# A 64-byte touch of batch 1's rows ahead of their load, in a transformer block on one core

## The chip, the core and the metric

The kernel runs on one core of a Trainium2 chip. The time is device microseconds of one execution. Each execution comes with a state, "fast" or "slow"; a lone execution on one core is "unknown". A profile is one further execution, taken by the hardware profiler; its span is about 2 us shorter than the device time. The sessions ran on different chips (the record names 12, 5, 10 and 0), so traces of different sessions can also differ by the chip.

## The reference, cut to what matters

```python
B, N, D = 2, 256, 1152                      # x: bf16[2, 256, 1152], c: bf16[2, 1152]
mod = (silu(c) @ w_mod).reshape(B, 6, 1, D) # shift_a, scale_a, gate_a, shift_m, scale_m, gate_m
h = layernorm(x) * (1 + scale_a) + shift_a
# q, k, v = h @ wqkv; attention with 2 heads; x = x + gate_a * (a @ wo)
# x + gate_m * (gelu(h2 @ w_fc1) @ w_fc2), h2 the second layernorm, modulated
```

Only the first line of the block matters here: x and c must arrive, x is normalised, transposed and scaled, and then the K projection can begin.

## The kernel before

x is held as four tiles of 128 partitions. Partition p of a batch holds rows 2p and 2p+1, so tiles 0 and 1 are the first and second row of each pair of batch 0, tiles 2 and 3 those of batch 1. A row is 2304 B, a pair 4608 B of contiguous memory.

```python
x_v = x.rearrange("b (p l) d -> p b l d", l=TPB)      # TPB = 2 rows to a partition
...
nc.scalar.dma_start(c_sb[:], c_v)                     # ACT's queue
for t in (0, 1, 3, 2):                                # SP's queue
    nc.sync.dma_start(x_sb[:, t, :], x_v[:, t // TPB, t % TPB, :])
... # then w_scale_a and w_k in pieces on SP's queue
nc.scalar.add_instruction(mybir.InstLoadActFuncSet(...))   # ACT's table load
warm(2, pwarm)                                        # TensorE matmuls on zeros
nc.tensor.transpose(pc[:], c_sb[:], ...)
nc.scalar.activation(sig[:], pc[:], ACT.Exp, scale=-1.0)   # silu(c), finished on DVE
...
warm(7, pwarm)
act_stats(0)                    # two ACT passes over tile 0: sum and sum of squares
for j in range(NPD): stats_piece(1, j)       # tile 1's statistics on DVE
act_mean_eps(0)
act_root(0)                     # inverse roots of tiles 0 and 1 on ACT: Ln, Ln, Exp
nc.scalar.activation(rstd1[:, 1:2], mv1[:, 1, 1:2], ACT.Ln, bias=eps_t[:], scale=1.0)
root_exp(0, 2)
act_stats(2)                    # two ACT passes over tile 2
for j in range(NPD): stats_piece(3, j)       # tile 3's statistics on DVE
...
norm1(1, 0, CUT); norm1(0, 0, CUT); pt_a = transpose_x([0, 1], BT[0])
act_mean_eps(2); act_root(2); root_exp(2, 3)
...
norm1(2, 0, CUT)
...
transpose_x([0, 1], [2], pt_c, 0)            # "tile 2's transposes" below
```

The kernel's last lines tie the instructions of each engine to the order of the text.

## Time and profile before

| what | before |
|---|---|
| time, median of 3 runs | 243.72 us (243.39 to 243.89) |
| span of the profile | 241.4 us |
| TensorE busy | 236.4 us (98%) |
| tile 2's transposes start | 11.03 us |
| x tiles 0, 1, 3, 2 land, us after their issues | 2.9, 3.2, 4.6, 4.9 |

The prediction shows the lines. Read them thus: the chain of waits says what ended last and what it had waited for, back to the start. It is on TensorE from 11.03 us to 238.3 us, so the time is 11.03 us plus a block on TensorE that this change does not edit. "Landing" is the time from the start of an issue until its semaphore says that all of it has arrived.

### The profile page before, as it was taken

The page shows a single profiled execution, that of the slowest core. Times are in us where ns is not written, and L with a number is a line of the kernel's source. Part 1 is how long each engine was busy: PE and PEld are TensorE (multiplying, and loading weights), DVE is VectorE, ACT ScalarE, POOL GpSimd, SP SyncE. Part 2 cuts the span into 40 slices and gives each one's busy share as a digit, 9 for nine tenths or more (in the row PEclk, how much of TensorE's full clock was granted, in tenths as well). Part 3 has the DMA queues.
Part 4 walks back from the last instruction along what each step waited for, and adds up shares of the span by engine and source line. Part 5 has one row for each costly group of instructions (what it writes and reads, how often), then busy time and mean ns, then how long its engine had stood idle before and what let it go on. Part 6 is the DMA issues. An engine that isn't in the chain of part 4 may idle for free.

```text
span 241.4 us, 3978 instructions
## 1 busy us (share of the span) xinstructions
PE 236.4 (98%) x1688; PEld 145.1 (60%) x1698; DVE 91.4 (38%) x193; ACT 59.9 (25%) x121; POOL 28.3 (12%) x47
## 2 busy tenths in 40 slices
PE   8999999999999999999999999999999999999994
PEld 5775444466667665888844444444665566666574
DVE  4842442319325678930003999950010000000001
ACT  6723322307215032770423333222000000000000
POOL 2300000001300324100000000001121111111111
PEclk9999999999999999999999999999999999999999
DMA  6999999997499993739999999999300000000000
GB/s 196 325 317 311 377 366 391 391 391 244 122 331 394 389 274 76 195 65 378 391 391 391 337 326 270 287 327 270 98 16 16 20 16 16 19 18 20 26 21 16
DMA packets 48781, 53.29 MB, mean 221 GB/s; under 512 B 9587, under 2 KB 36475, under 8 KB 48763
## 3 DMA queue, kind: packets, MB, share of 16 engines
q1 hardware_dynamic: 41312, 50.14, 62.5%
q10 hardware_dynamic: 6939, 1.71, 4.6%
q0 software_dynamic: 512, 1.19, 1.8%
q8 instruction: 13, 0.21, 0.4%
q14 instruction: 5, 0.04, 0.1%
HBM read 50.14 MB, written 1.19 MB: 213 GB/s over the span
## 4 chain that ended last, share of the span: by engine, by line
PE 94%; issue 2%; ACT 2%; POOL 1%; DVE 0%; POOLq 0%; DVEq 0%; ACTq 0%
PE pacc L802 29%; PE pacc L746 29%; PE pacc L693 7%; PE pacc L599 7%; PE pq L521 7%; PE pk L280 5%; PE pk L309 2%; PE pa L640 2%; PE ps_s L556 2%; PE pn L416 2%; ACT sink L206 1%; PE pt L264 1%; PE pm L247 1%; PE pg L498 0%; ACT rstd L335 0%
## 5 line engine op out<-in xcount | busy, mean ns | idle before, releaser
L746 PE MATMUL pacc<-hT,w_f 128*128 128x256 bf16 (+1 forms) x427 | 70.3, 325 | 0.3
L802 PE MATMUL pacc<-w_f,gT 128*128 128x384 bf16 (+2 forms) x468 | 70.5, 314 | 0.0
L802 PEld LDWEIGHTS <-gT 128*128 128x128 bf16 x468 | 44.4, 98 | 26.3
L746 PEld LDWEIGHTS <-w_f 128*128 128x128 bf16 x432 | 42.2, 98 | 27.6
L808 DVE TENSOR_TENSOR tmp<-pacc,gate 128x384 f32<-128x384 f32 (+2 forms) x13 | 6.8, 526 | 65.6 <-PE pacc L802 57.0
L778 ACT ACTIVATE gT<-pacc 128x512 bf16<-128x512 f32 x24 | 14.3, 597 | 32.7 <-PE pacc L746 32.7
L469 DVE SCALAR_TENSOR_TENSOR part<-w_gate_m,s,part 128x1152 f32<-128x1152 bf16 x16 | 21.4, 1412 | 0.0
L810 POOL TENSOR_TENSOR o_sb<-tmp,x 128x384 bf16<-128x384 f32 (+1 forms) x12 | 11.7, 972 | 53.9 <-DVE tmp L808 53.9
L693 PE MATMUL pacc<-w_o,big 128*128 128x384 bf16 x108 | 17.9, 326 | 0.0
L521 PE MATMUL pq<-hT,w_q 128*128 128x512 bf16 x79 | 17.7, 379 | 0.1
L599 PE MATMUL pacc<-w_v,hT 128*128 128x384 bf16 x108 | 17.7, 326 | 0.0
L599 PEld LDWEIGHTS <-hT 128*128 128x128 bf16 x108 | 10.5, 98 | 7.1 <-issue 0.2
L693 PEld LDWEIGHTS <-big 128*128 128x128 bf16 x108 | 10.4, 98 | 7.2 <-issue 0.4
L521 PEld LDWEIGHTS <-w_q 128*128 128x128 bf16 x81 | 7.8, 98 | 9.4
L280 PE MATMUL pk<-big,w_k 128*128 128x256 bf16 (+1 forms) x70 | 13.1, 324 | 0.1
L699 POOL TENSOR_TENSOR x<-tmp,x_sb 128x384 f32<-128x384 f32 x8 | 7.3, 912 | 27.0 <-DMA w_scale_m<-in_w_mod_dram 15.0
L467 DVE TENSOR_SCALAR part<-w_gate_m,s 128x1152 f32<-128x1152 bf16 x2 | 1.6, 818 | 21.9 <-DMA w_gate_m<-in_w_mod_dram 21.9
L491 POOL DMA_DIRECT2D gates_dram<-nat_v x2 | 1.1, 534 | 67.7 <-DVE nat_v L489 67.7
L280 PEld LDWEIGHTS <-w_k 128*128 128x128 bf16 x72 | 6.7, 97 | 3.7 <-issue 0.3
L767 ACT ACTIVATE gT<-pacc 128x512 bf16<-128x512 f32 x12 | 6.5, 598 | 9.1 <-PE pacc L746 9.1
L173 PE MATMUL pwarm<-zeros 128*128 128x256 f32 x18 | 7.4, 587 | 1.2 <-DVE eps_t L93 1.2
L512 POOL DMA_DIRECT2D gates_dram<-nat x4 | 2.4, 604 | 49.6 <-DVE nat L509 48.5
(102 smaller groups left out, 165.0 us busy)
## 6 DMA issues: line engine op xcount, KB each, us to landing
w_f<-in_w_fc_dram SPq DMA_DIRECT2D x12, 864.0 KB, 14.1
w_f<-in_w_fc_dram SPq DMA_DIRECT2D x3, 1728.0 KB, 7.9
w_f<-in_w_fc_dram SPq DMA_DIRECT2D x2, 2592.0 KB, 17.4
w_gate_a<-in_w_mod_dram SPq DMA_DIRECT2D x3, 864.0 KB, 12.1
w_v<-in_wqkv_dram SPq DMA_DIRECT2D x3, 864.0 KB, 13.8
w_o<-in_wo_dram SPq DMA_DIRECT2D x3, 864.0 KB, 14.0
w_shift_m<-in_w_mod_dram SPq DMA_DIRECT2D x3, 864.0 KB, 8.6
w_scale_m<-in_w_mod_dram SPq DMA_DIRECT2D x3, 864.0 KB, 13.3
```

The costliest lines, as they stand in the source:

```text
L173: nc.tensor.matmul(dst[:, 0:T // 2], zeros32[:, 0:P], zeros32, start=True, stop=True)
L280: nc.tensor.matmul(pk[m][:, c0:c1], w_k[:, k, m * P:(m + 1) * P], hT0[:, k, c0:c1], start=(k == 0 and c0 == 0), stop=(k == KD - 1), skip_g ...
L469: nc.vector.scalar_tensor_tensor(part[:, b, :], wg[:, k, :], s32[:, k, b:b + 1], part[:, b, :], op0=ALU.mult, op1=ALU.add,)
L521: nc.tensor.matmul(pq[m][:], w_q[:, k, m * P:(m + 1) * P], hT[:, k, :], start=(k == 0), stop=(k == KD - 1), skip_group_check=True,)
L599: nc.tensor.matmul(pacc[:], hT[:, k, t * P:(t + 1) * P], w_v[:, k, pnl * PW:(pnl + 1) * PW], start=(k == 0), stop=(k == KD - 1),)
L693: nc.tensor.matmul(pacc[:], aT[:, k, t * P:(t + 1) * P], w_o[:, k, c0:c1], start=(k == 0), stop=(k == KD - 1),)
L699: (nc.gpsimd if pool_add else nc.vector).tensor_tensor(x1[:, t, c0:c1], tmp[:], x_sb[:, t, c0:c1], op=ALU.add)
L746: nc.tensor.matmul(dst, w_f1[m // KD][:, k, ml * P:(ml + 1) * P], hT[:, k, c0:c1], start=start, stop=(k == KD - 1), **kw,)
L778: nc.scalar.activation(gT[:, m, :], pacc[:], ACT.Gelu_apprx_tanh)
L802: nc.tensor.matmul(pacc[:], gT[:, kk, t * P:(t + 1) * P], w_f2[j][:, r, c0 - n * PW:c0 - n * PW + cw], start=(kk == 0), stop=(kk == KF - 1),)
L808: nc.vector.tensor_tensor(tmp[:], pacc[:], gate_m[:, b, c0:c0 + cw], op=ALU.mult)
L810: (nc.vector if last else nc.gpsimd).tensor_tensor(o_sb[:], tmp[:], x1[:, t, c0:c0 + cw], op=ALU.add)
```

## The change

The intent is that a tiny read of each row pair of batch 1, in good time, makes the full read of those rows (tile 3, then tile 2) quicker.

```diff
     nc.scalar.dma_start(c_sb[:], c_v)
+    touch_x = act.tile([P, 32], BF16, name="touch_x")
+    nc.scalar.dma_start(touch_x[:], x_v[:, 1, 0, 0:32])
     for t in (0, 1, 3, 2):
```

Nothing reads `touch_x`.

## The prediction

> **What bounds the kernel now.** I read the page first, then the chain of waits in order of time, then the timeline of the first 12 us, then DMA traffic in short windows. The page says who is busy:
>
> ```profile
> span 241.4 us, 3978 instructions
> PE 236.4 (98%) x1688; PEld 145.1 (60%) x1698; DVE 91.4 (38%) x193; ACT 59.9 (25%) x121; POOL 28.3 (12%) x47
> PE 94%; issue 2%; ACT 2%; POOL 1%; DVE 0%; POOLq 0%; DVEq 0%; ACTq 0%
> ```
>
> The third line is the chain that ended last: 94% of the span is TensorE. The chain in order of time shows where the change can act:
>
> ```profile
> 6.51 0.29 ACT rstd L335
> ...
> 7.23 1.25 ACT sink L206 x2
> ...
> 10.56 0.42 DVE xn L233
> 10.98 0.05 issue
> 11.03 0.29 PE pt L264 x2
> 11.32 0.44 PE pk L280 x4
> ```
>
> The columns are start, length, what. From 11.03 us, where TensorE transposes the last tile of x, to 238.3 us the chain stays on TensorE, with some nine gaps of 0.05 us. The change touches only the prologue before 11.03 us. A microsecond lost or won at 11.03 is a microsecond at the end; nothing later can multiply it, and only about half a microsecond of gaps could hide it. So the stake is the few tenths by which that start moves.
>
> How x reaches the engines, from the timeline:
>
> ```profile
> 0.73 0.62 ACTq L84 DMA_DIRECT2D c_sb<-in_c_dram  x1
> 0.73 1.81 SPq L86 DMA_DIRECT2D x_sb<-in_x_dram  x4
> 1.39 1.28 ACT L153 ACT_TABLE_LOAD   x1 [1.39 <-PEq L841]
> 3.41 0.19 ACT L178 ACTIVATE sig<-pc 128x18 f32<-128x18 bf16 x1 [0.74 <-PE pc L176]
> 3.63 1.25 ACT L206 ACTIVATE sink<-x_sb 128x1152 f32<-128x1152 bf16 x1
> 4.38 1.48 DVE L193 BATCH_NORM_STATS2 stats<-x_sb 128x6 f32<-128x384 bf16 x3
> 6.22 1.48 DVE L193 BATCH_NORM_STATS2 stats<-x_sb 128x6 f32<-128x384 bf16 x3
> 7.13 1.24 ACT L206 ACTIVATE sink<-x_sb 128x1152 f32<-128x1152 bf16 x1
> ```
>
> The four x tiles are issued in the order 0, 1, 3, 2 about 0.45 us apart, and the tile view gives landings 2.9, 3.2, 4.6 and 4.9 us after issue: about 3.6, 4.4, 6.2 and 7.0 us. Their first readers start at 3.63 (ACT, tile 0), 4.38 (DVE, tile 1), 6.22 (DVE, tile 3) and 7.13 (ACT, tile 2). The landings thus sit within about 0.1 us of the readers, but no wait on x is listed: at each of the four points the reading engine had also just ended its previous work. Both conditions bind together.
>
> **What the Trainium skill says.** Four places bear on it.
> - "DMA: Bandwidth & Descriptors", section "Issuing engines are not separate DMA queues": loads from ACT and SP run on the same 16 engines and interleave. The trace agrees: c's 27 packets on queue q10 (18 rows and, I take it, 9 completion writes) lie among the first x packets on q1. So the touch is no free side channel.
> - The same page, "Queues, rings and completion order": an engine goes round-robin between the rows that have work, packet by packet. No run so far shows the order. By it the touch's 8 packets on each engine cut in among the packets of x tiles 0 and 1 though SP issued those first.
> - The same page, "Latency and other measured facts": HBM access 0.2 us on average, 2 us at high load, and about 0.8 us as the least round trip of a DMA. Here c's issue starts at 0.73 and its packets appear from about 1.6 us: 0.9 us, which fits. No page that I found says that a first read of an HBM row makes later reads of it faster.
> - "ScalarE: Activation LUTs", "What ACT_TABLE_LOAD costs": about 1283 ns for the load. The trace has 1.28 us. It stands right behind the DMA issue on ACT, so the new issue pushes it.
>
> **The change part by part.** It removes nothing. It adds one DMA issue on ACT, 128 reads of 64 B, 8 on each engine, a 64 B tile per partition that nobody reads, and perhaps a faster first read of batch 1's rows. A row pair is 2 x 2304 B = 4608 B, and tile 3 is the first tile to read them, tile 2 the second; likewise tile 0 and tile 1 for batch 0.
>
> *ACT issue.* c's issue took 0.62 us; an x issue of 128 rows on SP took 0.38 to 0.43. Take 0.45 to 0.65. The table load then runs from about 1.9 or 2.0 to 3.2 or 3.3 us. The next ACT instruction started at 3.41 after 0.74 us of idle time, waiting for PE, so the shift is covered with 0.1 to 0.3 us to spare: cost on the path 0. c is ahead on the same queue, and its packets were read by about 1.8 us, before the touch can start (1.4 issue + 0.9 = 2.3 us).
>
> *DMA work added.* c's packets of 256 B: 18 in the window 1.4 to 1.8 us, at a 3.9% share: 0.039 x 16 x 0.4 us / 18 = 14 ns each. If the touch's cost the same, 8 x 14 = 0.11 us on each engine. If each also carries a first-read penalty, more. That penalty I estimate from x's own packets of 2304 B, share x 16 x window / packets:
>
> ```profile
> q1 hardware_dynamic: 25, 0.06, 60.6%
> q1 hardware_dynamic: 74, 0.16, 103.7%
> q1 hardware_dynamic: 38, 0.07, 86.9%
> ```
>
> These are the windows 1.8 to 2.2 us (start of tile 0), 3.0 to 3.4 (tile 1) and 4.6 to 5.0 (tile 3). They give 155, 90 and 146 ns a packet. Batch 1's first reads do look some 60 ns slower than the second reads of batch 0's rows. That is presumably what the change is after. A touch packet could then take up to 14 + 60 = 74 ns, or 0.6 us an engine if nothing overlaps. Small reads should overlap in part; I choose 0.25 us as the delay that tiles 0 and 1 see, out of 0.1 to 0.6.
>
> *What the delay does.* Tile 1 lands at about 4.4 with its reader at 4.38: no slack. DVE's statistics of tile 1 (1.48 us), the aggregate and the small step at 6.05 feed POOL at 6.25, ACT at 6.51, then ACT's passes over tile 2 and DVE's at 10.56, which is the chain shown. Tile 0's delay is partly covered: ACT ended its second pass at 6.37 and started the next at 6.51, 0.14 us. So 0.25 us on tile 1 is about 0.2 us at 11.03.
>
> *What faster rows give back.* If tiles 3 and 2 (0.59 MB, from about 3.75 to 5.95 us by adding up the windows, 2.2 us) ran at tile 1's 369 GB/s they would need 1.6 us: at most 0.6 us earlier, which pays back the added packets and brings the weights behind them earlier. But on the chain it buys nearly nothing. Tile 3's reader is held by DVE until 6.14, tile 2's by ACT's exponential at 7.02: 0.08 and 0.1 us. An earlier tile 3 by itself shortens nothing on tile 1's path. The weights land at 8.98 (first scale chunk, used 9.04) and 9.6 (first K rows); earlier is of use only if TensorE is ready earlier, and it isn't, because it waits for the normalised tiles.
>
> *Sum.* +0.2 from tile 1, 0 from ACT, -0.05 from tile 3 and tile 2: about +0.15 us. 243.72 + 0.15 = 243.87, which I round to **243.9 us**.
>
> **The rivals.**
> 1. The warming works and pays: tiles 3 and 2 and the weights come 0.4 to 0.6 us earlier. For it: 146 against 90 ns a packet. Against it: at 6.22 and 7.13 the readers are bound by their own engines, and ACT's two passes over tile 2 (2.7 us) stay. If tile 1 is undisturbed it makes 243.4 to 243.7.
> 2. The touch is expensive: 64 B reads of cold rows hold their engines, tiles 0 and 1 land 0.6 us later and tile 2 too, since its slack is only 0.1 us. For it: all loads share the engines and tile 1 has no slack. Against it: c's 256 B packets took 14 ns. It makes 244.3 to 244.5.
> 3. The ACT issue is longer than 0.75 us because both queues generate descriptors at once; then the table load ends after 3.41 and the sigmoid of c slips, with DVE behind it, all on the path. c's 0.62 us against 0.38 on SP speaks for some of it. Each 0.1 us over costs 0.1: 243.9 to 244.2.
> 4. Nothing measurable: the touch overlaps entirely, 243.7.
>
> **Range and chances.** The three runs of before span 0.5 us by themselves. The mechanisms give from -0.3 to +0.8. The range that should hold it 8 times in 10 is 243.3 to 244.5. A change of 2% is 4.9 us, several times anything that the prologue can give: the whole stretch in which x is loaded and normalised is 11 us and the change adds 8 KB to it. So faster 0.01, within 2% 0.98, slower 0.01.
>
> **What would show it.** Right: the table load starts about 0.5 us later and the wait for PE before the sigmoid shrinks to 0.1 to 0.3; tile 1's statistics start 0.1 to 0.4 us after 4.38; the transposes of tile 2 start between 11.0 and 11.4 and the rest is shifted as a block. The warming is real if the packets at the start of tile 3 fall from about 146 to near 90 ns and tiles 3 and 2 take clearly under 4.6 and 4.9 us to land. Wrong: transposes of tile 2 starting before 10.9 us, which would mean that the landings, not the engines, set the readers; or after 11.6; or a difference that arises after 11.03 us, where I see no way for it.

## The result, and the profile after

| | before | after |
|---|---|---|
| median of 6 runs | 243.49 us (243.23 to 243.89) | 243.31 us (243.10 to 244.06) |
| ratio | | 0.9995, 95% interval 0.9978 to 1.0011 |
| span of the profile | 241.4 us | 241.4 us |

A ratio is the mean time of one kernel's fast runs over the mean of the other's of the same rounds, so it is not quite the ratio of the medians. The interval holds both the 0.15 us that I had forecast (1.0006) and a gain of that size. Time alone can say no more; what follows reads the start of the steady work in the traces.

The page of the changed kernel:

```profile
span 241.4 us, 3989 instructions
PE 236.6 (98%) x1698; PEld 144.9 (60%) x1698; DVE 91.5 (38%) x193; ACT 59.9 (25%) x121; POOL 28.3 (12%) x47
PE 94%; issue 2%; ACT 2%; POOL 1%; DVE 0%; POOLq 0%; DVEq 0%; ACTq 0%
```

The instruction counts differ by more than the one issue because some matmul records can be missing from a trace (1688 and 1698 here). Its timeline, in the lines that answer to those of before (the first two numbers are start and length):

```profile
1.38 0.36 ACTq L86 DMA_DIRECT2D touch_x<-in_x_dram  x1
1.78 1.28 ACT L155 ACT_TABLE_LOAD   x1 [1.78 <-issue]
3.41 0.19 ACT L180 ACTIVATE sig<-pc 128x18 f32<-128x18 bf16 x1 [0.35 <-PE pc L178]
4.42 1.48 DVE L195 BATCH_NORM_STATS2 stats<-x_sb 128x6 f32<-128x384 bf16 x3
6.10 1.47 DVE L195 BATCH_NORM_STATS2 stats<-x_sb 128x6 f32<-128x384 bf16 x3
7.18 1.24 ACT L208 ACTIVATE sink<-x_sb 128x1152 f32<-128x1152 bf16 x1
```

ACT's table load moved from 1.39 to 1.78 us; the sigmoid stayed at 3.41, and ACT's wait before it shrank from 0.74 to 0.35 us. Tile 1's statistics start 0.04 us later, tile 3's 0.12 us earlier, tile 2's 0.05 us later. In this trace tiles 3 and 2 landed 4.1 and 4.4 us after issue, each 0.5 us sooner than in the trace of before. The chain did not use it:

```profile
7.27 1.25 ACT sink L208 x2
...
10.60 0.42 DVE xn L235
11.03 0.05 issue
11.07 0.28 PE pt L266 x2
11.36 0.44 PE pk L282 x4
```

Tile 2's transposes start at 11.07 us against 11.03. ACT could begin tile 2 only when its own roots of tiles 0 and 1 were done. TensorE's first transposes, of tiles 1 and 0, came 0.13 us earlier (8.48 against 8.61 us); TensorE then sat idle for 0.30 us before tile 2's transposes, which ate that gain.

Where the touch's packets went is seen in the DMA traffic of 3.4 to 3.8 and 3.8 to 4.2 us (queue q10, which is ACT's; packets, MB, share of 16 engines' time):

```profile
q10 hardware_dynamic: 59, 0.00, 10.0%
q10 hardware_dynamic: 85, 0.00, 14.3%
```

These are all 144 packets that q10 gained: 128 reads of 64 B and 16 packets of 4 B, presumably completion writes (the packed trace lists the sizes). They took 0.143 x 16 x 0.4 us / 85 = 10.8 ns each, 0.1 us an engine in all. And they were served at 3.4 to 4.2 us. By 3.8 us q1 had moved 277 packets, and two tiles of x have 288 if each has 144 like the touch. So the touch ran at the end of tile 1 and the start of tile 3, which is the order of the issues (1.17 us tile 1, 1.38 touch, 1.62 tile 3), and at most some tenths of a microsecond ahead of the load that it should help.

### The profile page after: what moved, and what is told of

Its sections match the earlier page's. It is cut to its first block, busy times and chain, and to the rows that moved or that the text cites. A ratio compares the mean times of both kernels' runs of the same rounds, so it can differ in the third digit from the quotient of the medians.

```text
span 241.4 us, 3989 instructions
## 1 busy us (share of the span) xinstructions
PE 236.6 (98%) x1698; PEld 144.9 (60%) x1698; DVE 91.5 (38%) x193; ACT 59.9 (25%) x121; POOL 28.3 (12%) x47
## 4 chain that ended last, share of the span: by engine, by line
PE 94%; issue 2%; ACT 2%; POOL 1%; DVE 0%; POOLq 0%; DVEq 0%; ACTq 0%
PE pacc L748 29%; PE pacc L804 29%; PE pacc L695 7%; PE pacc L601 7%; PE pq L523 7%; PE pk L282 5%; PE pk L311 2%; PE pa L642 2%; PE ps_s L558 2%; PE pn L418 2%; ACT sink L208 1%; PE pt L266 1%; PE pm L249 1%; PE pg L500 0%; ACT rstd L337 0%
## 5 line engine op out<-in xcount | busy, mean ns | idle before, releaser
L748 PE MATMUL pacc<-hT,w_f 128*128 128x256 bf16 (+1 forms) x432 | 70.5, 326 | 0.0
L804 PE MATMUL pacc<-w_f,gT 128*128 128x384 bf16 (+2 forms) x468 | 70.5, 314 | 0.0
```

Of the source, the lines that this page charges most:

```text
L748: nc.tensor.matmul(dst, w_f1[m // KD][:, k, ml * P:(ml + 1) * P], hT[:, k, c0:c1], start=start, stop=(k == KD - 1), **kw,)
L804: nc.tensor.matmul(pacc[:], gT[:, kk, t * P:(t + 1) * P], w_f2[j][:, r, c0 - n * PW:c0 - n * PW + cw], start=(kk == 0), stop=(kk == KF - 1),)
```

## The experiments

The packets in 4.6 to 5.0 us, which the prediction took for the start of tile 3, gave the same picture. It shows the line of before (146 ns a packet); after has 108.9% x 6.4 us / 80 = 87 ns:

```profile
q1 hardware_dynamic: 80, 0.16, 108.9%
```

Two explanations stood against each other. **Warming**: the touch makes tiles 3 and 2 land 0.5 us sooner, and the order on ACT hides it. **Scatter**: landings differ by that much from run to run anyway. All fourteen traces with their prologues, so that they can be compared at once (landings in us after issue; the rest from the span's start):

| kernel | tile 3 lands | tile 2 lands | ACT starts tile 2 | tile 2's transposes | span |
|---|---|---|---|---|---|
| before | 4.6 | 4.9 | 7.13 | 11.03 | 241.4 |
| before_again | 4.3 | 4.8 | 7.17 | 11.06 | 241.7 |
| pool_only (no touch) | 4.3 | 4.8 | 6.97 | 11.08 | 241.4 |
| quiet (no touch at the start) | 4.1 | 5.0 | 7.10 | 11.01 | 241.8 |
| after | 4.1 | 4.4 | 7.18 | 11.07 | 241.4 |
| after_again | 4.4 | 5.6 | 7.74 | 11.66 | 242.0 |
| after_3 | 4.1 | 4.7 | 7.34 | 11.23 | 241.6 |
| pool_touch | 4.5 | 4.8 | 7.01 | 10.92 | 241.2 |
| touch_b0 | 3.9 | 5.0 | 7.19 | 11.09 | 241.4 |
| touch16 | 4.4 | 4.7 | 7.19 | 11.09 | 241.4 |
| touch3 | 4.7 | 5.1 | 7.67 | 11.57 | 242.3 |
| touch_first | 3.9 | 4.4 | 7.75 | 11.65 | 242.0 |
| touch_first2 | 3.9 | 4.5 | 7.76 | 11.96 | 242.3 |
| touch_first_b0 | 4.5 | 5.1 | 7.89 | 11.79 | 242.1 |

Span less the start of tile 2's transposes is 230.3 to 230.8 us in every row, while the start itself moves from 10.92 to 11.96: the start of the steady work sets the end to within half a microsecond, whatever the kernel. That half has causes of its own. In before_again, with 230.6, the chain does not lead back to x at all but to a piece of the weights behind it:

```profile
8.09 7.39 DMA w_scale_a<-in_w_mod_dram
15.52 0.60 PE pm L247 x18
```

In before these matmuls had started at 15.27 us.

### Both kernels again, unchanged

> The kernel before, unchanged, for the scatter of the landings. Warming theory (T1: the touch makes batch 1's rows faster to read): x tiles 3 and 2 land again 4.6 and 4.9 us after issue, within 0.15, and the packets in 4.6 to 5.0 us take 130 to 150 ns. Chance theory (T0: the 0.5 us between the two traces is scatter from run to run): one of the landings differs by 0.3 us or more from those. Transposes of tile 2 start at 11.03 within 0.1.

> The changed kernel, unchanged. T1: tiles 3 and 2 land 4.1 and 4.4 us after issue, within 0.15. T0: anything between 4.0 and 4.9. Transposes of tile 2 at 11.07 within 0.1 under both.

The repeat of before took 243.45 us, that of the changed kernel 243.77, and before on the same chip 243.98 (single runs, state unknown). In the repeat of the changed kernel tile 2 landed after 5.6 us, 1.2 us later than in its first trace, and this time it is on the chain:

```profile
2.11 5.61 DMA x_sb<-in_x_dram
7.72 0.02 issue
7.74 1.36 ACT sink L208 x2
...
11.66 0.29 PE pt L266 x2
```

The chain now leads back to the load of tile 2 itself (issued at 2.11 us), and the steady work starts 0.6 us late. The packets in 4.6 to 5.0 us, my measure of a slow first read, show the same scatter (the window also counts completion writes as packets, so it is a rough measure). These are q1's lines of that window in before_again and then in after_again:

```profile
q1 hardware_dynamic: 48, 0.09, 89.9%
q1 hardware_dynamic: 43, 0.08, 116.6%
```

That is 120 ns a packet without a touch and 174 ns with one, where the first pair of traces had 146 without and 87 with. Warming as I read it from one pair of traces fell here. In the repeat of before, tile 3 landed 0.3 us earlier than in its first trace, which the expectation had named as the sign of scatter. Its other part, transposes at 11.03 within 0.1, was met (11.06); for the changed kernel it was missed (11.66 against 11.07).

### Other rows, and fewer rows

```diff
-    nc.scalar.dma_start(touch_x[:], x_v[:, 1, 0, 0:32])
+    nc.scalar.dma_start(touch_x[:], x_v[:, 0, 0, 0:32])                   # touch_b0
+    nc.scalar.dma_start(touch_x[0:16, :], x_v[0:128:8, 1, 0, 0:32])       # touch16
```

> The same small load, but of batch 0's rows, which tile 0 has read by then. T1 (those rows of batch 1 must be touched): tiles 3 and 2 back at 4.6 to 4.7 and 4.9 to 5.0 us, since the load costs about 0.1 us an engine and warms nothing. Rival T2 (any small load queued between tiles 1 and 3 does it, for instance by spacing the queue): 4.1 and 4.4 as in the changed kernel. Tile 2's transposes between 11.0 and 11.2.

> A touch of every eighth row pair only, 16 reads onto 16 partitions. If what is warmed is a row pair or something of its size (T1a), tiles 3 and 2 land at 4.5 to 4.6 and 4.8 to 4.9 us, nearly as without a touch. If it is a stretch of memory of 36 KB or more (T1b), 4.0 to 4.2 and 4.3 to 4.5 as with the full touch. Tile 2's transposes between 11.0 and 11.15 in both.

With batch 0's rows touched, tile 3 landed after 3.9 us, as early as any in the table, and tile 2 after 5.0; with one pair in eight, 4.4 and 4.7. Neither pattern is that of either theory: the two tiles move apart from each other. The transposes started at 11.09 us in both. One look each (243.18 and 243.22 us, state unknown) cannot separate granularity from scatter, so touch16 settles nothing about the size of what might be warmed. The table does show that the chain keeps its start, 11.0 to 11.1 us, over landings of tile 2 from 4.4 (after) to 5.0 us (touch_b0, quiet).

### The changed kernel, timed once more

> The changed kernel a third time, with five rounds. The repeat landed tile 2 after 5.6 us where the first trace had 4.4, so T0 (scatter) leads: tile 2 anywhere from 4.4 to 5.6 us, and a time within 0.1% of before: ratio 0.999 to 1.001. If the touch really cost or gained 0.25 us, the ratio would be 1.001 or 0.999 and the interval, if it is as narrow as 0.1%, should tell.

Median 243.58 us against 243.54 for before, ratio 1.0002 (0.9976 to 1.0029). Tile 1 landed after 3.4 us and its statistics started at 4.58; the whole chain follows, with tile 2's transposes at 11.23. Over the four runs with the full touch in its place (after, after_again, after_3, pool_touch), tile 3 lands after 4.28 us in the mean and tile 2 after 4.88; over the four without a touch at the start, 4.33 and 4.88. No effect is left at this size of sample, though one of about 0.3 us on tile 3 could hide in it (my estimate, from its eight landings of 4.1 to 4.6 us). The packed traces allow a closer look, since they hold the duration of each packet. Take q1's reads of 2304 B in order of their start, 128 to a tile. Those of tile 3 took 149, 103, 121 and 123 ns in the mean without a touch, and 106, 146, 98 and 128 with it: 124 against 120 ns. Those of tile 0 took 117 to 140 ns, those of tile 1 93 to 114, and tile 0's were slower in each of the fourteen traces; tile 3's were slower than tile 2's in nine. So slower first reads stand in every trace for batch 0 alone, at the very start of the traffic, where the start itself may be the reason; for the rows that the touch is meant to help they come and go.

### Taking ACT's order away from in front of tile 2

The inverse roots of tiles 0 and 1 move to POOL, so that ACT can go straight from tile 0's passes to tile 2's, without the touch and with it.

```diff
-    act_mean_eps(0)
-    act_root(0)
-    nc.scalar.activation(rstd1[:, 1:2], mv1[:, 1, 1:2], ACT.Ln, bias=eps_t[:], scale=1.0)
-    root_exp(0, 2)
+    act_sq_mean(0)
+    nc.gpsimd.tensor_scalar_add(dm2[:, 0:1], dm2[:, 0:1], LN_EPS)
+    pool_eps(1)
+    nc.gpsimd.tensor_scalar(
+        mv1[:, 0, 1:2], dsq[:, 0:1], 1.0 / D, dm2[:, 0:1], op0=ALU.mult, op1=ALU.add
+    )
+    pool_rsqrt(0, 2)
+    act_mean(0)
```

> No touch. The inverse roots of tiles 0 and 1 move from ACT to POOL, so that ACT may begin tile 2's statistics when its first passes end at 6.4 us instead of 7.13. My theory of the end (the start of TensorE's steady work is set by the later of ACT's order and tile 2's landing at 7.0): ACT starts tile 2 at 7.0 on landing, names the load as what it waited for, and tile 2's transposes start at 10.9; time 0.1 us under before, ratio 0.9990 to 1.0005. Rival (ACT's order alone sets it, the landing has slack): ACT starts at 6.45 and the transposes at 10.7 or earlier, ratio 0.9985.

> The same move to POOL, with the touch. If the touch makes tile 2 land at 6.5 (as in the first trace of the changed kernel), ACT starts it at 6.5 and the transposes start at 10.7, 0.3 us before the kernel before: ratio 0.9988, and 0.2 us under pool_only. If the early landing was scatter (T0): a start anywhere from 6.5 to 7.7, and a ratio equal to pool_only's within 0.1%.

The timeline of pool_only and then of pool_touch, at ACT's first pass over tile 2:

```profile
6.97 1.26 ACT L206 ACTIVATE sink<-x_sb 128x1152 f32<-128x1152 bf16 x1 [0.60 <-DMA x_sb<-in_x_dram]
```

```profile
7.01 1.25 ACT L208 ACTIVATE sink<-x_sb 128x1152 f32<-128x1152 bf16 x1 [0.61 <-DMA x_sb<-in_x_dram]
```

With the roots gone, ACT waits 0.6 us for the load and starts only 0.16 to 0.17 us earlier than in before and after. So ACT's order and the load bound tile 2 within 0.2 us of each other, and an earlier landing could have been worth at most the 0.6 us of that wait. It did not come: tile 2 landed after 4.8 us in both, with the touch and without. The transposes start at 11.08 and 10.92 us: the first misses the 10.9 that I expected because tile 1 landed after 3.6 us and DVE began at 4.78, waiting 0.33 us for it. The chain of both kernels now runs from the landing of tile 1 through DVE's statistics and TensorE's own work, and no longer through tile 2. So in these two traces an earlier tile 2 would not have moved the start by itself.

The ratios are 0.9993 (0.9970 to 1.0016) and 0.9998 (0.9973 to 1.0022). The two ratios lie within the 0.1% that I expected, but their intervals are nearly 0.5% wide and could not have shown a difference of that size; and the version with the shortest span of all is not shown to beat either kernel.

### Three touches, to find ACT's slack

```diff
-    nc.scalar.dma_start(touch_x[:], x_v[:, 1, 0, 0:32])
+    for i in range(3):
+        nc.scalar.dma_start(touch_x[:, i, :], x_v[:, 1, 0, 0:32])
```

> Three touches in place of one, to find the slack on ACT. Each issue took 0.365 us and moved the table load by 0.39. With three it should start at 1.38 + 3 x 0.39 = 2.55 and end at 3.83, 0.45 us after the sigmoid's old start at 3.41 less its slack: sigmoid at 3.85, tile 1's statistics at 4.85, tile 2's transposes at 11.5, ratio 1.0015 to 1.0025. Rival (the issue and the table load overlap, or the slack is larger): sigmoid stays at 3.41 and tile 2's transposes at 11.1 to 11.2, ratio under 1.001.

The timeline of ACT:

```profile
1.38 1.32 ACTq L87 DMA_DIRECT2D touch_x<-in_x_dram  x3
2.73 1.28 ACT L156 ACT_TABLE_LOAD   x1 [2.73 <-issue]
4.03 0.19 ACT L181 ACTIVATE sig<-pc 128x18 f32<-128x18 bf16 x1
```

The later issues took 0.44 and 0.45 us, so the table load moved to 2.73 us, 0.18 beyond what I expected, and the sigmoid to 4.03: no wait for PE is left in front of it. Tile 2's transposes start at 11.57 us, 0.5 us after the changed kernel's first trace. The time was 244.03 to 244.18 us in four runs, ratio 1.0017, though with 0.9986 to 1.0048 the interval still holds 1. The slack of 0.74 us on ACT is real and finite: the table load moved by 1.34 us and the sigmoid by 0.62, so 0.72 us were absorbed. One touch fits in it, three do not.

### The touch ahead of c

```diff
-    nc.scalar.dma_start(c_sb[:], c_v)
     touch_x = act.tile([P, 32], BF16, name="touch_x")
     nc.scalar.dma_start(touch_x[:], x_v[:, 1, 0, 0:32])
+    nc.scalar.dma_start(c_sb[:], c_v)
```

> The touch ahead of c on the same queue. In the changed kernel its packets were served at 3.4 to 4.2 us, right before tile 3's, so it could hardly warm anything in time; here they should come at about 1.6 us, 2 us ahead of tile 3. T1' (rows can be warmed, the touch only came too late): tile 3 lands after 4.0 us or less and tile 2 after 4.4 or less, and packets in 4.6 to 5.0 us take about 90 ns. T0 (no warming, the landings scatter): tile 3 at 3.9 to 4.7, tile 2 at 4.4 to 5.6. c comes 0.4 us later in both; if its slack under TensorE's warm-up matmuls is over 0.4, the sigmoid stays at 3.41. Ratio 0.999 to 1.002.

> The same kernel again, for the scatter. T1': tiles 3 and 2 within 0.15 us of the run before it and at 4.0 and 4.4 or less. T0: one of the two differs from that run by 0.2 us or more, or both are as without a touch.

> The touch ahead of c as in the two runs before it, but of batch 0's rows, so that nothing of batch 1 is touched. Those two landed tile 3 after 3.9 us and tile 2 after 4.4 and 4.5, the earliest pair of all. If that is because batch 1's rows had been touched (T1'), tiles 3 and 2 fall back to 4.2 to 4.6 and 4.7 to 5.0. If it has nothing to do with the rows (the order of the issues, or chance), they stay at 3.8 to 4.1 and 4.3 to 4.6. The sigmoid at 4.1 and the span at 242.0 in both.

The 171 packets of q10, the touch's and c's together, came at 1.8 to 3.4 us, 100 of them at 2.6 to 3.0 in touch_first, and not at 1.6. That is at the end of tile 0, issued at 0.73 us like the touch, and about a microsecond earlier than in the changed kernel. Both runs that touched batch 1's rows landed tile 3 after 3.9 us and tile 2 after 4.4 and 4.5; the one that touched batch 0's rows 4.5 and 5.1. The direction is that of warming by an early touch. But it rests on two runs against one, and that one ran on another chip in a later session; quiet, which has no touch at the start and shared the chip of the two, landed tile 3 after 4.1 us. touch_b0 had 3.9 without touching tile 3's rows, and the packets in 4.6 to 5.0 us took 70.5% x 6.4 us / 34 = 133 ns in the first of the two and 109 in the second, not the 90 that warming should give. I leave it open.

What it costs in the trace is plain. The chain of touch_first begins with c:

```profile
1.19 2.64 DMA c_sb<-in_c_dram
3.83 0.05 issue
3.87 0.19 PE pc L178
4.07 5.45 PE pwarm L175 x14
9.51 0.22 PE pt L266 x4
```

c landed at 3.83 us, the sigmoid slipped to 4.10 to 4.24, and the steady work started at 11.65 to 11.96. The chain does not pass through the sigmoid: the 14 warm-up matmuls that stand behind c's transposition on TensorE slip with it, and they took 5.45 us here and 5.93 in the second run. ACT's start of tile 2 came 0.6 us late as well, so both ways lead to about the same time, and in touch_first_b0 the chain is that of ACT. c had no slack to speak of, where I had named 0.4 us as the condition; in the trace of before, the transposition had already waited 0.65 us for it. The five timed runs gave 243.78 us against 243.60, ratio 1.0005 (0.9992 to 1.0019): the 0.6 us of the trace are not shown in the time. The nine runs of before in that session had spans of 241.7 to 242.1 us, as long as the 241.9 to 242.0 of touch_first.

### The loads by themselves, on quiet queues

The kernel before, with ten loads one after the other near the end. DVE clears the destination first, which sets the moment; each load writes the same tile and so waits for the one before.

```diff
         nc.sync.dma_start(out_v[:, b, t % TPB, c0:c0 + cw], o_sb[:])
+        if gi == 5:
+            quiet = act.tile([P, D], BF16, name="quiet")
+            nc.vector.memset(quiet[:], 0.0)
+            nc.scalar.dma_start(quiet[:], x_v[:, 1, 0, :])           # first
+            nc.scalar.dma_start(quiet[:], x_v[:, 1, 0, :])           # repeat
+            nc.scalar.dma_start(quiet[:, 0:32], x_v[:, 0, 0, 0:32])  # touch
+            nc.scalar.dma_start(quiet[:], x_v[:, 0, 0, :])           # touched
+            nc.scalar.dma_start(quiet[:], x_v[:, 0, 0, :])           # repeat
+            ... # the same five on rows of wo
```

> The kernel before, with ten extra loads one after the other on ACT's queue at about 203 us, when the queues are nearly idle: a 288 KB tile of x last read 200 us ago, the same again at once, a 64 B touch of other rows, those rows in full, the same again; then the same five on rows of wo. Each waits for the one before. T1: a first read takes longer than its repeat by 0.3 us or more, and a touched one is as short as a repeat. T0: all full loads take the same from issue to landing, about 2.5 to 2.9 us, within 0.15; the touches about 1.9.

```profile
204.43 0.37 ACTq L817 DMA_DIRECT2D quiet<-in_x_dram  x1
207.63 0.33 ACTq L818 DMA_DIRECT2D quiet<-in_x_dram  x1
210.78 0.34 ACTq L819 DMA_DIRECT2D quiet<-in_x_dram  x1
212.84 0.34 ACTq L820 DMA_DIRECT2D quiet<-in_x_dram  x1
215.61 0.34 ACTq L821 DMA_DIRECT2D quiet<-in_x_dram  x1
219.28 0.33 ACTq L822 DMA_DIRECT2D quiet<-in_wo_dram  x1
222.00 0.34 ACTq L823 DMA_DIRECT2D quiet<-in_wo_dram  x1
225.15 0.34 ACTq L824 DMA_DIRECT2D quiet<-in_wo_dram  x1
226.74 0.33 ACTq L825 DMA_DIRECT2D quiet<-in_wo_dram  x1
229.54 0.33 ACTq L826 DMA_DIRECT2D quiet<-in_wo_dram  x1
```

The distance from one issue to the next is a load's whole time. First reads (of rows not read for a long while) took 3.20 and 2.72 us, touched ones 2.77 and 2.80, repeats 3.15, 3.67, 3.15 and 3.0 (the last by its landing); the two touches 2.06 and 1.59. A read repeated at once is no quicker than a first read, against the warming theory. My expectation for scatter was too tight as well: equal loads of 288 KB differ by almost a microsecond here, though the kernel's own stores run beside them.

## Why the prediction was right, point by point

- **The stake is only the prologue: right.** The steady work took 230.3 to 230.8 us in every trace. I saw no way for a difference after 11.03 us; before_again has one, of about 0.2 us, in its wait for weights at 15.5 us.
- **The number: right, with luck.** I forecast a slowdown of 0.15 us. The median fell by 0.18 us and lies 0.01 us above the lower end of my range of 243.3 to 244.5. The six runs of before alone span 0.66 us, so the time speaks neither for my sign nor against it.
- **ACT's issue costs nothing on the path: right.** The issue took 0.365 us where I took 0.45 to 0.65; the slack left is 0.35 us, a little over the 0.1 to 0.3 that I had named. The three touches show that it is slack, since they overran it.
- **The touch's work on the engines: right at 0.1 us, wrong in what I made of it.** A packet took 10.8 ns against the 14 ns of c's. The step that failed is "I choose 0.25 us as the delay that tiles 0 and 1 see". Its ground, a first-read penalty of 60 ns that each touch packet would carry, is not in the packets; and they ran at the end of tile 1, not among tiles 0 and 1. I had taken the single reads that the trace calls packets for the larger packets of the round-robin that I cited (the last section returns to this). I had also read c's packets as done by about 1.8 us, though 9 of its 27 stand in the two windows after that. Tile 1 landed after 3.2, 3.3 and 3.4 us in the changed kernel, and after 3.1 to 3.6 in the four without a touch. So the +0.15 us of the sum was a delay that the runs do not show apart from this scatter.
- **The slow first reads of batch 1: not shown.** I read 146 against 90 ns off one trace, and had picked the windows: in 3.4 to 3.8 us of that same trace, still tile 1's, a packet took 137.2% x 6.4 us / 69 = 127 ns. Nor is 4.6 to 5.0 us the start of tile 3: q1 had moved 396 packets before it, and three tiles have 432, so it is the end. In the window of 4.6 to 5.0 us four traces without the touch give 104 to 146 ns, and four with it 87 to 174. That differs from run to run, whichever the kernel. Whether a touch that comes much earlier would warm anything is open.
- **Earlier rows buy nearly nothing: right for what the trace showed.** Tiles 3 and 2 did land 0.5 us earlier in the first trace, and the start moved from 11.03 to 11.07. pool_only and pool_touch then confirm that ACT's order and the landing stand within 0.2 us of each other.
- **What I left out.** I gave tile 2 a slack of 0.1 us and did not ask how much its landing scatters. In the repeat it came 1.2 us later, and 0.6 us of that went to the end. That is larger than any cost or gain of the touch that the runs show. My list of signs counted a start after 11.6 us as proof against the prediction; the repeat had 11.66 with the load of tile 2 as its cause, which no sum of mine contained.

## What to carry to other kernels

Before a slow stretch in one trace is given a cause, take the trace of the same kernel a second time: here the 0.5 us that the first pair of traces showed was inside the scatter of one load. A load that should prepare another must be served well before it, and in these traces it was served at its place in the order of issue, although it stood on another queue. And a load that lands earlier is worth only the wait of its reader: look first whether the reader's own engine is free.

## What the Trainium skill lacked or had wrong

- "DMA: Bandwidth & Descriptors", section "Queues, rings and completion order", has an engine go round-robin between the queues with work, a whole packet of some 9 to 17 descriptors at a time. These runs do not contradict it, since the touch's share of an engine is only 9 of the trace's packets (144 on 16 engines). What the page lacks is when a queue counts as having work. Here whole loads followed each other in the order of issue across the two queues: the touch, issued at 1.38 us, came at 3.4 to 4.2 us, between tiles 1 and 3 of SP's queue; put ahead of c, 100 of that queue's 171 packets came at 2.6 to 3.0 us, at the end of tile 0. Whether the engines or the making of the descriptors set this order is not shown.
- No page has the scatter of a load's landing: the same 288 KB load, tile 2 in the five traces of the two kernels, landed 4.4 to 5.6 us after issue, and equal loads on nearly idle queues took 2.7 to 3.7 us from one issue to the next.
- No page says whether a recent read of the same rows makes a read quicker. On nearly idle queues four repeats took 3.0 to 3.7 us and two first reads 2.7 and 3.2, so none was seen there; in the prologue it stays open.
